# The attention bias in scratch memory laid out so that one read of 128 partitions brings a part of the bias tile for both blocks of rows, the first part read one round sooner

## The chip, the cores and the metric

The kernel runs on one core of a Trainium2 chip. The metric is the device time of one execution in microseconds (us), lower is better. Its engines, as the profile names them: PE (TensorE, matmuls; PEld is its weight loads), DVE (VectorE), ACT (ScalarE), POOL (GpSimd) and SP, which computes nothing here and issues every DMA.

## The reference, cut to what matters

```python
batch, n_heads, seq, head_dim = (4, 8, 576, 64)
...
scores = scale * np.matmul(q, k.transpose(0, 1, 3, 2))
rel = (pos[:, None] - pos[None, :]).astype(np.float32)
x = (np.log1p(np.abs(rel)) / psi_i)[..., None]
h = np.maximum(x @ w1 + b1, 0.0)
bias = h @ w2
scores = scores + bias.transpose(2, 0, 1)[None, :, :, :]
scores = scores - np.max(scores, axis=-1, keepdims=True)
attn = np.exp(scores)
attn = attn / (np.sum(attn, axis=-1, keepdims=True) + 1e-09)
out = np.matmul(attn, v)
```

The bias of a head is a 576 x 576 matrix that a small network computes from the distance of two positions and the row's position; all four batches share it. The attention's output goes through a feed-forward layer (512 to 2048 to 512) and then through a soft mixture of 8 experts; neither is touched here.

## The kernel before, in words

**The bias stage (`bias_phase`, to about 70 us).** The 576 positions of the query are cut into 9 blocks of 64 rows. Blocks c and 8 - c (c = 0 to 3) go as a pair over 128 partitions, one of them on the even and the other on the odd partitions; block 4 goes alone, with its own scratch tensor `W4`. A round k (0 to 8) makes 64 distances: PE multiplies masks with weights (L160), DVE makes of the sums the bias values of 64 distances forwards (L193) and POOL copies them in reverse order for the distances backwards (L211). They collect in SBUF tiles called `rows`, with two heads (a head pair, hp = 0 to 3) interleaved. When the last round of a chunk of distances is done (`CHUNKS`), `put` (L220) sends the chunk to the scratch tensor `W` in HBM, by `send` (L215, the DMA on line L216). `W` holds for each row a line of 1152 distances for each of two heads, so a shifted window of 576 of them is that row's bias. Pair c = 3 is complete after round 5, c = 2 after round 6, c = 1 after round 7 and c = 0 after round 8. For c < 3 the last chunk (for c = 0 also the one before it) is sent for head pair 0 alone, and the rest of it (`late`, 8 DMAs) after everything else.

**The reads.** `bias_rows` (L324) reads the windows back into a bias tile `nb` of 128 partitions and 9 x 576 values: part s (0 to 3) holds the pair c = 3 - s, part 4 the block 4 of both heads. Before, one part takes two DMAs of 64 rows: one of the first block of the pair into the even partitions and one of the other block into the odd ones. For head pair 0 the parts are read one by one (`bias_first`, L349): part 0 and part 4 after round 6, part 1 after round 7, parts 2 and 3 after the last round. For head pairs 1 to 3 `load` (L357) reads all parts when the first batch of that head pair is loaded.

**Attention (`Attention.run`, L544).** There are 16 pairs of head pair and batch. Each has 9 score tiles of 128 x 576, t = 0 to 8: `scores` (L414, PE), `least` (L437, DVE: adds the bias from `nb`, scales and takes the row's minimum of the negated sum, giving z), `power` (L457, ACT: the exponential e), `transposes` (L477, PE) and `gather` (L491 on DVE, L493 on ACT: g), then `pv` (L505, PE) and small sums (`inverse`, L523). `SLOT` says which rows of the bias tile a score tile takes: t = 0 and 1 take part 0, t = 2 and 3 part 1, t = 4 and 5 part 2, t = 6 part 4, t = 7 and 8 part 3. The order is written out in `ROUND`: round i ends pair i and begins pair i + 1. The inputs q and k of pair i + 2 (`raw`, L365) are loaded in round i, and POOL splits them into two parts each (`split`, L382 and L384: qh, kh, ql, kl). PSUM has 4 buffers for score and transposed tiles together, so PE stops where DVE does not take a score tile.

**Queues.** All DMAs go through SP, which works in program order; a DMA whose condition is not met holds all those behind it. Their completions are counted on eight semaphores that are used in turn (DMAHW0 to DMAHW7 below).

Of the kernel before, what the change touches and what calls it, by code (L numbers as in the profile page):

```python
# [8 lines left out]
F32 = mybir.dt.float32  # L9
# [10 lines left out]
P = 128  # L20
B, H, S, D = 4, 8, 576, 64
HP = H // 2
# [15 lines left out]
PITCH = 2 * S  # L38
# [30 lines left out]

def bias_phase(tc, ident, W, W4, cpack, lcol, prow, xmain, xtail, att):  # L70


    nc = tc.nc
    with ExitStack() as ctx:
# [73 lines left out]
        def unit(k, c):  # L148

            if c < 4 or k % 2 == 0:  # L150
                accs[c] = ap_.tile([P, 2, 2, H, 32], F32, tag="acc", name=f"acc{k}_{c}")
            acc = accs[c]
            if c < 4:
                m, cols, dst = P, slice(P * c, P * c + P), acc
            else:
                m, cols = 64 * (k % 2) + 64, slice(512, S)
                dst = acc[m - 64 : m]
            for u in range(16):
                for part in range(3):
                    nc.tensor.matmul(  # L160
                        dst[:, u // 8, :, :, 4 * (u % 8) : 4 * (u % 8) + 4],
                        mask[:, (16 * k + u) % RING, cols],
                        wp[:, part],
                        start=part == 0,
                        stop=part == 2,
                    )
            if c == 4 and k in (0, 2):
                return
            ks = CHUNKS[c]
            i = max(n for n in range(len(ks)) if ks[n] <= k)  # L170
            d0, w, f0 = 64 * ks[i], 64 * (ks[i + 1] - ks[i]), 64 * (k - ks[i])
            last = k + 1 == ks[i + 1]
            if c == 4:
                w, f0, xs = 64, 0, xt_t[:m, i]
            else:
                xs = xm_t[:, k, c]
            if f0 == 0:
                tag = TAGS[c][i]
                rows[c] = fps[tag].tile([P, H * 2 * w], F32, tag=tag, name=f"rows{c}_{i}")
            mine = rows[c]  # L180
            if c == 4:
                both = rows[c].rearrange("p (h x) -> p h x", h=H).unsqueeze(2)
            else:
                both = rows[c].rearrange("p (a x b) -> p a b x", a=HP, b=2)
            fwd = both[:m, :, :, w + f0 : w + f0 + 64]
            tmp = cp.tile([P, H, 2, 32], F32, tag="tmp", name=f"tmp{k}_{c}", bufs=2)
            xb = xs.rearrange("p (s j) -> p s j", s=2).unsqueeze(1).to_broadcast([m, H, 2, 32])
            a0, a1 = (acc[:m, :, n].rearrange("p s h j -> p h s j") for n in range(2))
            nc.vector.tensor_tensor(tmp[:m], a0, xb, ALU.mult)
            if c == 4:  # L190
                nc.vector.tensor_tensor(fwd[:, :, 0].rearrange("p h (s j) -> p h s j", s=2), tmp[:m], a1, ALU.add)
            else:
                nc.vector.tensor_tensor(  # L193
                    fwd.rearrange("p a b (s j) -> p a b s j", s=2),
                    tmp[:m].rearrange("p (a b) s j -> p a b s j", b=2),
                    a1.rearrange("p (a b) s j -> p a b s j", b=2),
                    ALU.add,
                )

            one = d0 == 0 and c < 4  # L200
            z = int(one and f0 == 0)
            a = both[:m, :, :, w + one - f0 - 64 : w + one - f0 - z]
            if c == 4:
                a, src = a[:, :, 0], fwd[:, :, 0]
            else:
                src = fwd[:, :, :, z:]
            e = a.ap[-1][0]
            back = bass.AP(
                tensor=a.tensor, offset=a.offset + (63 - z) * e, ap=[list(v) for v in a.ap[:-1]] + [[-e, 64 - z]]
            )  # L210
            nc.gpsimd.tensor_scalar(back, src, 1.0, 1.0, ALU.mult, ALU.mult)  # L211
            if not last:
                return

            def send(dst, src, pin):  # L215
                i = nc.sync.dma_start(dst, src)  # L216
                if pin:
                    tc.keep_in_program_order(i)

            def put(half, blk, d0, n_r, n_l, one, hs):  # L220

                q = slice(64 * half, 64 * half + 64) if blk == 4 else slice(half, P, 2)
                if blk == 4:
                    e, dst = 1, W4.rearrange("h p j -> p h j")
                else:
                    e = 2
                    dst = W[blk - (blk > 4) if blk > 4 else 3 - blk, hs].rearrange("a p j b -> p a (j b)")
                src = mine.rearrange("p (h x) -> p h x", h=H // e)[:, hs if e == 2 else slice(0, H)]

                def move(j0, x0, n):  # L230
                    send(dst[:, :, e * j0 : e * (j0 + n)], src[q, :, e * x0 : e * (x0 + n)], k > 4)

                if one:
                    move(S - n_l, w - n_l + 1, n_l + n_r - 1)
                    return
                if n_r > 0:
                    move(S - 1 + d0, w, n_r)
                if n_l > 0:
                    y = int(d0 == 0)
                    move(S - d0 - n_l, w - n_l, n_l - y)  # L240

            def flush(hs):
                if c == 4:
                    for half in range(m // 64):
                        put(half, 4, d0 + 64 * half, 64, 64, False, hs)
                else:
                    far, near = min(w, S - 64 * c - d0), max(0, min(w, 64 * c + 64 - d0))
                    put(0, c, d0, far, near, one, hs)
                    put(1, 8 - c, d0, near, far, one, hs)

            if c < 3 and (k + 1 == ks[-1] or c == 0 and i == 2):
                flush(slice(0, 1))
                late.append(lambda: flush(slice(1, HP)))
            else:
                flush(slice(0, HP))
# [8 lines left out]
        for k in range(NG):  # L264
            cs = [c for c in range(3, -1, -1) if k <= NG - 1 - c]
            if k < 5:
                cs.append(4)
            done = 0
            for n_, c in enumerate(cs):
                unit(k, c)  # L270
                if k + 1 < NG:
                    upto = 16 * (n_ + 1) // len(cs)
                    for u in range(done, upto):
                        make_mask(k + 1, u)
                    done = upto
            if k < 4:
                att.split(0, k)
            if k in (6, 7):
                att.bias_first(k - 6)
        att.load(1)  # L280
        att.load_v(1)
        att.bias_first(2)
# [5 lines left out]
class Attention:  # L288
# [17 lines left out]

    def __init__(self, tc, ident, W, W4, xT, rs, qk, v_l):
        self.tc, self.nc, self.ident = tc, tc.nc, ident
# [15 lines left out]
    def bias_rows(self, hp, s, n):  # L324

        nb = self.nb[hp]
        if s == 4:
            parts = [(slice(64 * par, 64 * par + 64), 4) for par in range(2)]
        else:
            parts = [(slice(q, P, 2), s + 5 * q) for q in range(2)]  # L330
        for p, blk in parts:
            i0 = 64 * (blk if blk >= 4 else 3 - blk)
            if s == 4:
                a = self.W4[2 * hp + p.start // 64, :, S - 1 - i0 : 2 * S - 1 - i0]
                src = bass.AP(tensor=a.tensor, offset=a.offset, ap=[[PITCH - 1, 64], [1, S]])
                dst = nb[p, 8 * S :]
            else:
                a = self.W[blk - (blk > 4), hp, :, S - 1 - i0 : 2 * S - 1 - i0]
                step = H * 64 * PITCH + (128 if blk < 4 else -128)
                dims = [[2 * (PITCH - 1), 64], [step, n], [1, 2 * S]]  # L340
                src = bass.AP(tensor=a.tensor, offset=a.offset, ap=[d for d in dims if d[1] > 1])
                dst = nb[p, 2 * S * s : 2 * S * (s + n)]
                if n > 1:
                    dst = dst.rearrange("p (s x) -> p s x", s=n)
            i = self.nc.sync.dma_start(dst, src)
            if hp == 0:
                self.tc.keep_in_program_order(i)
# [824 lines left out]
def kernel(  # L1172
# [1 line left out]
):  # L1174
    nc = tc.nc
    dram = ctx.enter_context(tc.tile_pool(name="scratch", bufs=1, space=DRAM))
    W = dram.tile([8, HP, 64, PITCH, 2], F32, name="W")
    W4 = dram.tile([H, 64, PITCH], F32, name="W4")
    xT = dram.tile([HP, P, N], F32, name="xT")
    rs = dram.tile([H, N], F32, name="rs")  # L1180
# [4 lines left out]
    att = Attention(tc, ident, W, W4, xT, rs, qk, v_l)  # L1185
# [9 lines left out]
    x0 = ctx.enter_context(tc.tile_pool(name="m_x0", bufs=1, reuse_waits="tile"))  # L1195
# [179 lines left out]
```

## Time and profile before

| | |
|---|---|
| time, median of 3 runs | 819.85 us (819.35 to 821.1) |
| the profiled execution's own time | 815.85 us |
| its span, first to last instruction | 813.9 us |
| mean granted clock of TensorE | 0.975 of full speed |
| busy: PE, DVE, ACT, POOL | 759.6, 546.7, 495.1, 314.5 us |
| HBM read and written | 91.95 and 21.29 MB |
| reads of the bias tile | 6 of 1152 KB, 8 of 288 KB, 8 of 144 KB |

PE is busy for 93% of the span and is on the chain that ended last for 45% of it, mostly in the feed-forward layer (L725, L753). In the row of 40 slices (each 20.3 us) PE is at 9 tenths or more nearly everywhere after the first 15% of the span; the one slice before that where it falls to 3 tenths is the fourth, 61 to 81 us, where the bias stage ends and attention begins. The granted clock falls in the same place, and the DMA share there is high.

### The profile page before, as it was taken

How to read it: one execution, taken by the hardware profiler on the slowest of the kernel's cores; microseconds unless marked ns; L12 is line 12 of the kernel's file. 1: busy time of each engine (PE TensorE's matmuls, PEld its weight loads, DVE VectorE, ACT ScalarE, POOL GpSimd, SP SyncE). 2: the span in 40 equal slices, each digit the busy share in tenths (PEclk: the TensorE clock that was granted, in tenths of full speed). 3: DMA queues.
4: the chain of work that ended last, by engine and by line, in shares of the span. 5: the costliest groups of instructions: out<-in, count | busy, mean ns of one | idle time of the engine just before them, and what ended most of it. 6: DMA issues, size and time to landing. Idle time of an engine off the chain costs nothing.

```text
span 813.9 us, 18359 instructions
## 1 busy us (share of the span) xinstructions
PE 759.6 (93%) x7428; PEld 634.7 (78%) x7428; DVE 546.7 (67%) x958; ACT 495.1 (61%) x974; POOL 314.5 (39%) x239
## 2 busy tenths in 40 slices
PE   6993599999999999999999999999999999998993
PEld 6883477787877778988898988888888899886342
DVE  6894688888988856777778565655675656465103
ACT  8980688888888853443346566656566556655002
POOL 4742225375646623113224454445543641141000
PEclk9998799999999999999999999999999999999897
DMA  6596923738535542332340011301100124339986
GB/s 198 168 276 199 372 79 121 272 108 308 171 95 177 181 137 78 140 120 104 104 130 1 1 33 40 136 1 40 39 1 20 39 104 130 104 104 328 384 351 232
DMA packets 49669, 114.44 MB, mean 141 GB/s; under 512 B 10544, under 2 KB 29872, under 8 KB 47536
## 3 DMA queue, kind: packets, MB, share of 16 engines
q1 hardware_dynamic: 49584, 113.26, 41.3%
q8 instruction: 58, 0.95, 0.5%
q14 instruction: 27, 0.22, 0.1%
HBM read 91.95 MB, written 21.29 MB: 139 GB/s over the span
## 4 chain that ended last, share of the span: by engine, by line
PE 45%; DVE 3%; ACT 1%; DMA 1%; POOL 1%; issue 0%; DVEq 0%; ACTq 0%
PE h L725 18%; PE ys L753 18%; PE hps L1136 2%; PE ops L1136 2%; PE lp L823 1%; DMA em<-in_mw_dram 1%; PE turn L1145 1%; PE o L1163 1%; DVE x L644 0%; DVE g L736 0%; PE sp L882 0%; PE sp L883 0%; DVE wr L685 0%; DVE gr L741 0%; PE tl L870 0%
## 5 line engine op out<-in xcount | busy, mean ns | idle before, releaser
L736 DVE SCALAR_TENSOR_TENSOR g<-g,nal 128x384 f32<-128x384 f32 x96 | 100.6, 1048 | 83.9 <-ACT g L735 83.5
L437 DVE CUSTOM_DVE_ANT_0 z<-s,nb 128x576 f32<-128x576 f32 x144 | 108.2, 755 | 26.0 <-DMA W<-rows 12.6
L457 ACT ACTIVATE e<-z,m 128x576 f32<-128x576 f32 x144 | 109.9, 766 | 6.2 <-DVE m L437 6.2
L739 ACT ACTIVATE gr<-g 128x384 fp32r<-128x384 f32 x96 | 50.2, 523 | 86.7 <-DVE g L736 86.6
L505 PE MATMUL o<-g,v 128*64 128x256 f32 (+1 forms) x640 | 86.4, 415 | 0.5 <-ACT g L493 0.5
L493 ACT ACTIVATE g<-t 128x640 f32<-128x640 f32 x96 | 67.2, 702 | 31.1 <-PE t L477 26.8
L733 ACT ACTIVATE g<-h 128x384 f32<-128x384 f32 x96 | 46.8, 488 | 54.5 <-PE h L725 51.4
L414 PE MATMUL s<-kh,qh 64*128 64x288 f32 x320 | 61.3, 379 | 16.4 <-DVE m L437 14.9
L741 DVE TENSOR_TENSOR gr<-g,gr 128x384 fp32r<-128x384 f32 x80 | 53.8, 673 | 33.2 <-ACT gr L739 33.2
L477 PE MATMUL t<-ident,e 64*128 64x64 f32 x1440 | 67.9, 223 | 3.7 <-ACT g L493 3.2
L477 PEld LDWEIGHTS t<-ident,e 64*128 64x128 f32 x1440 | 65.7, 139 | 5.3 <-ACT g L493 3.9
L160 PE MATMUL acc<-wp,mask 128*128 128x64 bf16 (+1 forms) x1680 | 56.4, 197 | 11.2 <-DVE mask L144 5.2
L505 PEld LDWEIGHTS o<-g,v 128*64 128x64 f32 x640 | 43.9, 138 | 29.0 <-ACT g L493 1.0
L160 PEld LDWEIGHTS <-mask 128*128 128x128 bf16 (+1 forms) x1680 | 54.2, 103 | 13.3 <-DVE mask L144 5.2
L142 ACT ACTIVATE mask<-pr,wb 128x576 bf16<-128x576 f16 (+4 forms) x94 | 54.6, 677 | 2.5 <-PE acc L160 2.5
L382 POOL TENSOR_SCALAR qh<-raw 128x1216 fp32r<-128x1216 f32 x16 | 19.4, 1211 | 87.4 <-PE s L414 67.1
L414 PEld LDWEIGHTS s<-kh,qh 64*128 64x128 f32 x320 | 31.1, 190 | 25.4 <-DVE m L437 15.6
L741 POOL TENSOR_TENSOR gr<-g,gr 128x384 fp32r<-128x384 f32 x16 | 19.1, 1194 | 77.8 <-ACT gr L739 39.3
L414 PE MATMUL s<-kl,qh 64*128 64x288 f32 x320 | 48.0, 295 | 0.0
L414 PE MATMUL s<-kh,ql 64*128 64x288 f32 x320 | 47.8, 294 | 0.0
L735 ACT ACTIVATE g<-h 128x384 f32<-128x384 f32 x96 | 46.5, 485 | 0.0
L384 POOL TENSOR_TENSOR ql<-raw,qh 128x1216 fp32r<-128x1216 f32 x16 | 44.8, 2801 | 0.0
(990 smaller groups left out, 2016.7 us busy)
## 6 DMA issues: line engine op xcount, KB each, us to landing
wide<-in_w_dram SPq DMA_DIRECT2D x16, 1024.0 KB
ep<-in_mw_dram SPq DMA_DIRECT2D x29, 512.0 KB
raw<-in_qk_dram SPq DMA_DIRECT2D x16, 896.0 KB
nb<-W SPq DMA_DIRECT2D x6, 1152.0 KB
v<-in_v_l_dram SPq DMA_DIRECT2D x16, 320.0 KB
pre<-in_mw_dram SPq DMA_DIRECT2D x10, 512.0 KB
ex<-in_mw_dram SPq DMA_DIRECT2D x9, 512.0 KB
em<-in_mw_dram SPq DMA_DIRECT2D x8, 512.0 KB
```

Source lines behind the costliest of these rows:

```text
L142: nc.scalar.activation(dst, pr[:, :n], AF.Sigmoid, bias=wb[:, t : t + 1], scale=BIG)
L160: nc.tensor.matmul(dst[:, u // 8, :, :, 4 * (u % 8) : 4 * (u % 8) + 4], mask[:, (16 * k + u) % RING, cols], wp[:, part], start=part == 0, ...
L414: nc.tensor.matmul(s[:, hf, :288], st["q", a][d, o : o + P], st["k", b][d, 288 * h : 288 * h + 288], start=n_ == 0, stop=n_ == len(seq) - 1,),
L437: self.nc.vector.tensor_tensor_reduce(out=z.rearrange("p (a b) -> p a b", a=2), in0=s[:, :, :288], in1=nb.rearrange("p (a b) -> p a b", a= ...
L457: self.nc.scalar.activation(e, z, AF.Exp, bias=m, scale=-1.0, accum_out=st["sum"][:, slot : slot + 1]),
L477: self.pin(i, nc.tensor.transpose(tp[:, r, 64 * c : 64 * c + 64], e[q, k0 : k0 + P], self.ident[q, q]))
L493: self.pin(i, nc.scalar.activation(dst, src, AF.Copy))
L505: nc.tensor.matmul(op[64 * h : 64 * h + 64, 0, :n], st["v"][:, h, c], g[:, h, c], start=c == 0, stop=c == 4),
L725: nc.tensor.matmul(h, w_[:, c * P : (c + 1) * P], x_[:, c], start=c == 0 and n_ == 0, stop=c == NC - 1 and n_ == 2,)
L736: nc.vector.scalar_tensor_tensor(g, neg, self.nal[:, f : f + 1], g, ALU.mult, ALU.add)
L741: eng.tensor_tensor(gl, g, gh.bitcast(F32), ALU.subtract)
L753: i = self.nc.tensor.matmul(self.ys[blk][t], g_[:, t * P : (t + 1) * P], w_[:, 512:], start=f == 0 and n_ == 0, stop=f == NF - 1 and n_ == 2,)
```

## The change

It lays `W` out anew: for each pair c and head pair 128 lines of 2304 values, in the order of the partitions, so that the lines of the two blocks alternate. The line of the second block is shifted by 256 (4 - c) - 1 values (an odd number of words), so that a window that moves back by one value from one line to the next fits both blocks. Then one DMA of 128 rows reads one part. `put` writes into every second line. `bias_first(0)` is called after round 5 in place of round 6, so part 0 and part 4 are read one round sooner; the other parts stay where they were.

```diff
@@ put @@
-                    e, dst = 1, W4.rearrange("h p j -> p h j")
+                    e, odd, dst = 1, 0, W4.rearrange("h p j -> p h j")
                 else:
-                    e = 2
-                    dst = W[blk - (blk > 4) if blk > 4 else 3 - blk, hs].rearrange("a p j b -> p a (j b)")
+                    e, odd = 2, half * (256 * (4 - c) - 1)
+                    dst = W[3 - c, hs, half::2].rearrange("a p j -> p a j")
...
-                    send(dst[:, :, e * j0 : e * (j0 + n)], src[q, :, e * x0 : e * (x0 + n)], k > 4)
+                    send(dst[:, :, e * j0 + odd : e * (j0 + n) + odd], src[q, :, e * x0 : e * (x0 + n)], k > 4)
@@ the rounds @@
-            if k in (6, 7):
-                att.bias_first(k - 6)
+            if k in (5, 7):
+                att.bias_first(k // 7)
@@ bias_rows, parts 0 to 3 @@
-                a = self.W[blk - (blk > 4), hp, :, S - 1 - i0 : 2 * S - 1 - i0]
-                step = H * 64 * PITCH + (128 if blk < 4 else -128)
-                dims = [[2 * (PITCH - 1), 64], [step, n], [1, 2 * S]]
+            x0 = 2 * (S - 1 - 64 * (3 - s))
+            a = self.W[s, hp, :, x0 : x0 + 2 * S]
+            dims = [[2 * PITCH - 1, P], [HP * P * 2 * PITCH + P, n], [1, 2 * S]]
...
-                dst = nb[p, 2 * S * s : 2 * S * (s + n)]
+            dst = nb[:, 2 * S * s : 2 * S * (s + n)]
@@ the scratch tensor @@
-    W = dram.tile([8, HP, 64, PITCH, 2], F32, name="W")
+    W = dram.tile([4, HP, P, 2 * PITCH], F32, name="W")
```

In the order of the built program PE, DVE, ACT and POOL keep theirs through attention and the feed-forward layer. Three places matter here. In the names, `rows3_2` is the third chunk of pair c = 3, `W_57` is `W`, `W4_58` is `W4`, `nb0` the bias tile of head pair 0, and the brackets give what the instruction waits for.

SP, the end of round 5 and round 6, before:

```order
L216 DMA W_57<-rows3_2_1363 64x4x256 [waits DMAHW6_49]
L216 DMA W_57<-rows1_2_1478 64x4x256 [waits DMAHW7_49,Pool_49]
L216 DMA W_57<-rows1_2_1478 64x4x256 [waits DMAHW0_49]
L216 DMA W_57<-rows2_2_1711 64x256 [waits DMAHW1_49,Pool_49]
L216 DMA W_57<-rows2_2_1711 64x256 [waits DMAHW2_49]
L216 DMA W_57<-rows0_2_1535 64x384 [waits DMAHW3_49,Pool_49]
L216 DMA W_57<-rows0_2_1535 64x384 [waits DMAHW4_49]
L345 DMA nb0_2016<-W_57 64x1152 [waits DMAHW5_49]
L345 DMA nb0_2016<-W_57 64x1152 [waits DMAHW6_49]
L345 DMA nb0_2016<-W4_58 64x576 [waits DMAHW7_49]
```

and with the change:

```order
L216 DMA W_57<-rows3_2_1363 64x4x256 [waits DMAHW6_49]
L216 DMA W_57<-rows1_2_1478 64x4x256 [waits DMAHW7_49,Pool_49]
L216 DMA W_57<-rows1_2_1478 64x4x256 [waits DMAHW0_49]
L343 DMA nb0_1836<-W_57 128x1152 [waits DMAHW6_49,DMAHW5_49,DMAHW1_49]
L343 DMA nb0_1836<-W4_58 64x576 [waits DMAHW4_49,DMAHW3_49,DMAHW2_49]
L343 DMA nb0_1836<-W4_58 64x576
L216 DMA W_57<-rows2_2_1711 64x256 [waits Pool_49]
L216 DMA W_57<-rows2_2_1711 64x256
L216 DMA W_57<-rows0_2_1535 64x384 [waits Pool_49]
```

The two DMAs of part 0 became one, and it and those of part 4 now stand ahead of the four writes of round 6. It waits for the two writes of `rows3_2`, the last of pair c = 3.

SP, from the writes of round 7 to the last reads, before:

```order
L216 DMA W_57<-rows1_3_1945 64x256 [waits DMAHW1_49,Pool_49]
L216 DMA W_57<-rows1_3_1945 64x256 [waits DMAHW2_49]
L345 DMA nb0_2016<-W_57 64x1152 [waits DMAHW3_49]
L345 DMA nb0_2016<-W_57 64x1152 [waits DMAHW4_49]
L216 DMA W_57<-rows0_3_2133 64x256 [waits DMAHW5_49,Pool_49]
L216 DMA W_57<-rows0_3_2133 64x256 [waits DMAHW6_49]
L345 DMA nb0_2016<-W_57 64x1152 [waits DMAHW7_49,DMAHW1_49]
L345 DMA nb0_2016<-W_57 64x1152 [waits DMAHW2_49,DMAHW0_49]
L345 DMA nb0_2016<-W_57 64x1152 [waits DMAHW5_49]
L345 DMA nb0_2016<-W_57 64x1152 [waits DMAHW6_49]
L216 DMA W_57<-rows2_2_1711 64x3x256 [waits DMAHW3_49]
```

and with the change:

```order
L216 DMA W_57<-rows1_3_1949 64x256 [waits DMAHW0_49,Pool_49]
L216 DMA W_57<-rows1_3_1949 64x256 [waits DMAHW1_49]
L343 DMA nb0_1836<-W_57 128x1152 [waits DMAHW5_49,DMAHW4_49,DMAHW2_49]
L216 DMA W_57<-rows0_3_2132 64x256 [waits DMAHW3_49,Pool_49]
L216 DMA W_57<-rows0_3_2132 64x256
L343 DMA nb0_1836<-W_57 128x1152 [waits DMAHW1_49,DMAHW0_49]
L343 DMA nb0_1836<-W_57 128x1152 [waits DMAHW6_49,DMAHW7_49,DMAHW4_49,DMAHW3_49]
L216 DMA W_57<-rows2_2_1711 64x3x256 x2
```

Each part is one read; the read of part 1 still stands behind the writes of `rows1_3`, that of part 2 behind those of `rows0_3`, and that of part 3 waits for the latter.

DVE, the first tiles of attention (the z of pair 0), before:

```order
L437 ISA z0_0_2264,m0_0_2265<-s0_0_2257,nb0_2016 128x576 [waits DMAHW3_49,DMAHW4_49,DMAHW2_49,DMAHW5_49,DMAHW1_49,DMAHW6_49,DMAHW0_49,DMAHW7_49,PE_49,Activation_49]
L437 ISA m0_0_2265 128x1
L437 ISA z0_1_2274,m0_1_2275<-s0_1_2267,nb0_2016 128x576 [waits PE_49]
L437 ISA m0_1_2275 128x1
L437 ISA z0_2_2286,m0_2_2287<-s0_2_2277,nb0_2016 128x576 [waits PE_49]
L437 ISA m0_2_2287 128x1
L437 ISA z0_3_2300,m0_3_2301<-s0_3_2291,nb0_2016 128x576 [waits PE_49]
L437 ISA m0_3_2301 128x1
L437 ISA z0_4_2310,m0_4_2311<-s0_4_2303,nb0_2016 128x576 [waits PE_49]
```

and with the change:

```order
L435 ISA z0_0_2260,m0_0_2261<-s0_0_2253,nb0_1836 128x576 [waits DMAHW1_49,PE_49,Activation_49]
L435 ISA m0_0_2261 128x1
L435 ISA z0_1_2270,m0_1_2271<-s0_1_2263,nb0_1836 128x576 [waits PE_49]
L435 ISA m0_1_2271 128x1
L435 ISA z0_2_2282,m0_2_2283<-s0_2_2273,nb0_1836 128x576 [waits DMAHW2_49,PE_49]
L435 ISA m0_2_2283 128x1
L435 ISA z0_3_2296,m0_3_2297<-s0_3_2287,nb0_1836 128x576 [waits PE_49]
L435 ISA m0_3_2297 128x1
L435 ISA z0_4_2306,m0_4_2307<-s0_4_2299,nb0_1836 128x576 [waits DMAHW5_49,PE_49]
L435 ISA m0_4_2307 128x1
L435 ISA z0_5_2329,m0_5_2330<-s0_5_2309,nb0_1836 128x576 [waits PE_49]
L435 ISA m0_5_2330 128x1
```

Before, the first z waits for all eight DMA semaphores, and the next ones for none. Now the first waits for one, that of the read of part 0; the z of t = 2 and t = 4 each wait for one more, that of their own part, and so do those of part 4 and part 3 behind them.

## Rows read from the trace of the kernel before

**Rows 1.** The bias tile's instructions, what they wait for (all of the span).

```profile
L437 DVE CUSTOM_DVE_ANT_0 z<-s,nb x144: 697/758/760, 82.8 to 293.1; 128x576 f32<-128x576 f32 x144
L345 SPq DMA_DIRECT2D nb<-W x22: 451/601/1332, 68.5 to 197.5; - x22
...
  DMA W<-rows: 12.6, 1
```

**Rows 2.** DVE's instructions in order: start us, us, line, tiles, [idle <-releaser].

```profile
69.52 0.69 DVE L193 TENSOR_TENSOR rows<-tmp,acc 128x512 f32<-128x512 f32 x1
...
82.79 0.76 DVE L437 CUSTOM_DVE_ANT_0 z<-s,nb 128x576 f32<-128x576 f32 x1 [12.59 <-DMA W<-rows]
...
85.51 0.75 DVE L437 CUSTOM_DVE_ANT_0 z<-s,nb 128x576 f32<-128x576 f32 x1
...
91.53 0.75 DVE L437 CUSTOM_DVE_ANT_0 z<-s,nb 128x576 f32<-128x576 f32 x1
...
93.22 2.52 DVE L523 SCALAR_TENSOR_TENSOR r<-sum 128x9 f32<-128x9 f32 x1 [0.94 <-ACT e L457]
...
95.90 0.70 DVE L437 CUSTOM_DVE_ANT_0 z<-s,nb 128x576 f32<-128x576 f32 x1
...
111.36 0.76 DVE L437 CUSTOM_DVE_ANT_0 z<-s,nb 128x576 f32<-128x576 f32 x1
...
124.38 0.76 DVE L437 CUSTOM_DVE_ANT_0 z<-s,nb 128x576 f32<-128x576 f32 x1
```

**Rows 3.** Busy us of each engine by stretch, then granted clock, DMA share, GB/s.

```profile
42.00:60.00 18.00, 16.30 (x525) 15.60 (x522) 17.34 (x38) 16.19 (x35) 7.08 (x11) 1.00 0.96 268
...
74.00:82.00 8.00, 0.00 (x0) 0.00 (x0) 0.00 (x0) 0.00 (x0) 0.00 (x0) 0.50 0.88 288
82.00:87.00 5.00, 2.97 (x26) 2.63 (x28) 4.16 (x12) 3.37 (x6) 0.00 (x0) 0.50 1.08 330
...
98.00:102.00 4.00, 3.79 (x28) 2.48 (x30) 0.69 (x3) 2.37 (x6) 0.00 (x0) 0.59 1.05 352
```

**Rows 4.** SP's DMAs in order: start, us of issuing, line, tiles.

```profile
61.21 2.27 SPq L216 DMA_DIRECT2D W<-rows  x2
...
73.90 1.17 SPq L216 DMA_DIRECT2D W<-rows  x2
...
77.00 1.09 SPq L345 DMA_DIRECT2D nb<-W  x2
78.13 5.84 SPq L216 DMA_DIRECT2D W<-rows  x8
84.01 0.69 SPq L365 DMA_DIRECT2D raw<-in_qk_dram  x1
...
165.05 1.82 SPq L623 DMA_DIRECT2D xb<-rs  x2
```

**Rows 5.** POOL's instructions in order, as rows 2.

```profile
68.37 1.29 POOL L211 TENSOR_SCALAR rows<-rows 128x512 f32<-128x512 f32 x2 [1.08 <-DVE rows L193]
70.29 0.67 POOL L211 TENSOR_SCALAR rows<-rows 128x512 f32<-128x512 f32 x1 [0.62 <-DVE rows L193]
91.15 1.21 POOL L382 TENSOR_SCALAR qh<-raw 128x1216 fp32r<-128x1216 f32 x1 [20.20 <-PE s L414]
...
92.97 2.74 POOL L384 TENSOR_TENSOR ql<-raw,qh 128x1216 fp32r<-128x1216 f32 x1
95.67 1.41 POOL L384 TENSOR_TENSOR kl<-raw,kh 128x576 fp32r<-128x576 f32 x1
...
169.57 1.02 POOL L634 TENSOR_TENSOR xu<-xu,xb 128x384 f32<-128x384 f32 x1 [1.09 <-DMA xb<-rs]
```

**Rows 6.** ACT's instructions in order, as rows 2.

```profile
88.73 0.76 ACT L457 ACTIVATE e<-z,m 128x576 f32<-128x576 f32 x1
...
89.48 0.68 ACT L493 ACTIVATE g<-t 128x640 f32<-128x640 f32 x1
```

**Rows 7.** Line L523 in all pairs: min/median/max ns of one.

```profile
L523 DVE SCALAR_TENSOR_TENSOR r<-sum x16: 166/718/2517, 93.2 to 295.3; 128x9 f32<-128x9 f32 x16
```

More of the change, by code (lines that the diff above doesn't have):

```diff
@@ L326, in bias_rows @@
         nb = self.nb[hp]
+        jobs = []
         if s == 4:
-            parts = [(slice(64 * par, 64 * par + 64), 4) for par in range(2)]
-        else:
[L330 to L337, printed above, removed]
-                a = self.W[blk - (blk > 4), hp, :, S - 1 - i0 : 2 * S - 1 - i0]
-                step = H * 64 * PITCH + (128 if blk < 4 else -128)
-                dims = [[2 * (PITCH - 1), 64], [step, n], [1, 2 * S]]
-                src = bass.AP(tensor=a.tensor, offset=a.offset, ap=[d for d in dims if d[1] > 1])
-                dst = nb[p, 2 * S * s : 2 * S * (s + n)]
-                if n > 1:
-                    dst = dst.rearrange("p (s x) -> p s x", s=n)
+            for par in range(2):
+                a = self.W4[2 * hp + par, :, S - 1 - 256 : 2 * S - 1 - 256]
+                src = bass.AP(tensor=a.tensor, offset=a.offset, ap=[[PITCH - 1, 64], [1, S]])
+                jobs.append((nb[64 * par : 64 * par + 64, 8 * S :], src))
+        else:
+            x0 = 2 * (S - 1 - 64 * (3 - s))
+            a = self.W[s, hp, :, x0 : x0 + 2 * S]
+            dims = [[2 * PITCH - 1, P], [HP * P * 2 * PITCH + P, n], [1, 2 * S]]
+            src = bass.AP(tensor=a.tensor, offset=a.offset, ap=[d for d in dims if d[1] > 1])
+            dst = nb[:, 2 * S * s : 2 * S * (s + n)]
+            if n > 1:
+                dst = dst.rearrange("p (s x) -> p s x", s=n)
+            jobs.append((dst, src))
+        for dst, src in jobs:
             i = self.nc.sync.dma_start(dst, src)
```

## The prediction

> **What bounds the kernel now.** I read four views in this order. First what the bias tile waits for [rows 1]: 144 z instructions on DVE read it, and one single wait of 12.6 us stands before them, put down to a DMA. Then DVE in order of time [rows 2]: DVE ends the bias stage at 69.52 + 0.69 = 70.21, and the first z starts at 82.79, after 12.59 us of idle time. The table by stretch [rows 3] shows that this is a hole in the whole kernel: from 74 to 82 no engine does anything, the DMA queue is busy at a share of 0.88, and TensorE's granted clock is 0.50 of full speed, the lower level of 1.2 GHz; it is still 0.50 from 82 to 87, when PE works again. Last SP's order [rows 4]: the last two reads of the bias tile are issued from 77.00 to 78.09, then the eight late writes, then `raw` of pair 2 at 84.01.
>
> The built order says what the first z waits for: before, all eight DMA semaphores, which covers the ten reads of all parts, though it needs part 0 alone. The next z's wait for no DMA, and they do follow each other without a gap (82.79 to 85.51 are four z's in 2.7 us [rows 2]). So the start of attention is set by the last read, not by the first. With the change the first z waits for one read. That is what the time should come from; the fewer DMAs as such matter less.
>
> **The change part by part.**
>
> *When part 0 is there.* Its read stands behind the writes of round 5, whose issue ends at 61.21 + 2.27 = 63.48 [rows 4], and waits for writes that were issued a few us sooner. How long a write takes to land: the read at 77.00 waited for the first of the writes issued from 73.90 [rows 4], so 3.1 us at most there. The queue was fuller in 42 to 60 (share 0.96 [rows 3]), so the read may go out at 63.5, or up to 2 us later. How long a 128-row read takes no row shows. Below: the second `xb` read, issued at 165.05 + 1.82 - 0.6 = 166.27 [rows 4], released POOL at 169.57 [rows 5], 3.3 us for a much smaller read. Above: the second of the last reads, issued at about 77.5 [rows 4], was followed by z at 82.79 [rows 2], 5.3 us with writes beside them. I take 4.0, nearer the lower end, because at 63.5 little else is in the queue. Part 0 is there at 67.5 (66.8 to 70.8), and the first z can start when DVE is free, at 70.3: 12.5 us sooner (12.0 at the worst end).
>
> *Parts 1 to 3.* They now pace the first pair. POOL ends the rows of round 7 by 69.66 and those of round 8 at 70.96 [rows 5]. SP writes the former from 69.0 to 70.2, then issues the read of part 1: landed at 74.2. It writes the latter to 72.1; the read of part 2 waits for the writes of round 7 (69.6 + 3.1 = 72.7): landed at 76.7. The read of part 3 waits for the writes of round 8 (71.6 + 3.1 = 74.7): landed at 78.7. Each may be 0.7 us less or 1.3 us more.
>
> *To the end of pair 0's z's.* The first z of part 2 is at 76.7 instead of 85.51 [rows 2]. Its second ends at 78.2, and ACT, which now keeps up, computes the sixth e (0.76 us, before at 88.73 [rows 6]) to 79.0. From the end of that e at 89.49 (where ACT's g follows, then PE's transposes and its last score tile) the last z took 2.04 us before, to 91.53. So the last z is at 81.0, later than part 3 needs: **10.5 us sooner**.
>
> *The gap before pair 1.* Before, DVE's r at 93.22 took 2.52 us, while the median of r is 0.72 [rows 2, 7]; POOL's ql ran from 92.97 to 95.71 [rows 5] and r ended with it. With the change POOL cannot be there yet, since it waits for `raw` of pair 2 (below). That gives back 1.8 us (2.35 at most, by the shortest r of 0.17): **1.8 us**, so that pair 1's first z is at 83.6 rather than 95.90.
>
> *Pair 1.* Before, pair 1 took 111.36 - 95.90 = 15.46 us where pair 2 took 124.38 - 111.36 = 13.02 [rows 2]. The excess of 2.4 lies where the clock fell once more (0.59 in 98 to 102 [rows 3]). Whether it falls again is open: the gain is 0 to 2.4, and I take **1.2**, half.
>
> *`raw` of pair 2.* The late writes follow the last read, now at 74.7 and 0.6 us long instead of to 78.09: `raw` is issued some 2.8 us sooner, at 81.2. Before, POOL started on it at 91.15, waiting for PE's last score of pair 0 and not for the DMA [rows 5], so it lands at most 7.1 us after its issue: by 88.3. POOL's four splits take 97.08 - 91.15 = 5.93, to 94.3, and pair 2's first z can follow a score tile later, some 95.1. The sum puts it at 111.36 - 13.5 = 97.9, so this does not bind; it caps the gain at 16.3.
>
> *The rest.* The other head pairs' reads are three DMAs instead of four, each hidden: pair 4 needs its bias 26 us after pair 2 starts. From pair 2 on the rounds are 13 us and the orders are the same, so what is gained by pair 2's first z is kept to the end. Writes are as many and as long as before; that they go to every second line I cost at nothing, which the fourth rival below takes up.
>
> Sum: 10.5 + 1.8 + 1.2 = **13.5 us**. The profiled execution's own time, 815.85, becomes 802.35. The median of the runs, 819.85, stands 4.0 above it and includes the same hole; taken off there, 806.35, say **806.3 us**.
>
> A rule speaks for another sum. The trace's part first: the two reads of a part were issued one after the other, each by itself, and z waited for the last of ten [rows 1, 4]. The Trainium skill (DMA: Bandwidth & Descriptors, Rules for kernel authors) says that two transfers to disjoint halves of the partitions serialise, because both use the same 16 engines, and that one transfer of 128 partitions should be used. By that rule the merged read moves the same bytes over the same engines and saves an issue, some 0.6 us each, about 2 us of SP's time up to the last read; the sum would be 2 to 3 us. It says nothing of what a reader waits for, and the order does.
>
> **The rivals.**
>
> *The clock stays low and the first pair starves.* The z's come in twos, each two behind a read, so PE works in short bursts from 71 to 79. For it: the clock was at 0.50 after one hole of 12 us and fell to 0.59 again when PE was only partly busy before 98 [rows 3]. At half clock the score tile and transposes ahead of the last z cost some 1 us more, part 1 to 3 may each come 1.3 late, and pair 1 keeps its 15.46: 10.5 - 2.3 + 1.8 = 10, so 809.9. The Trainium skill (TensorE: Matmul & The Clock Gate, HAM oscillation) describes such a loop of bursts and DMA waits, with the clock low again at each burst. The trace agrees as far as a long hole goes; no row shows short ones.
>
> *The first z is held by the writes, as the view names them.* The idle time is put down to W<-rows, not to the reads. If the eight late writes hold z, the change moves them only as far as the last read, 2.8 to 3.3 us: 816.8. Against it: in the order z waits for nothing that stands behind the reads; the semaphores are used in turn by reads and writes, which is how the name can be wrong.
>
> *More is gained.* Pair 1 runs at 13 us and r at its shortest: up to the cap of 16.3, 803.5.
>
> *Slower: the odd lines cost.* The second block's runs now begin at an odd word and go to every second line. The queue is busy 0.96 of the 18 us from 42 to 60 [rows 3], in which SP issued nothing but writes of `W` and `W4`. If the second block's half of them took twice as long, 0.96 x 18 / 2 = 8.6 us would be added there, and half of the 5.84 of the late writes [rows 4], 2.9: 11.5 against a gain of 13.5, still 2 us faster. It decides from a factor of 2.2; at three times it is 23 - 13.5 = 9.5 slower, 829. No row excludes it, but the reads of block 4 already step by an odd number of words, and nothing waits for them alone.
>
> **How the numbers follow.** Forecast (10.5 to 15 us gained): 0.67. Low clock (8.5 to 10.5): 0.15. Writes hold z: 0.06. More than 15: 0.07. Odd lines at twice the time or more: 0.05, of it 0.02 within what can be told and 0.03 slower. The range takes in the first, most of the second and the larger gains up to 18 (cap 16.3 and the spread of the runs, 1.7): 801.8 to 811.4. A change of under 0.2%, 1.6 us, can't be told from none here: faster by more 0.95, within 0.02, slower 0.03.
>
> **What would show it.** The first z at 70 to 71 us; gaps before the z's of t = 2 and 4, at about 74 and 77, put down to reads of the bias tile; the last z of pair 0 near 81, pair 1's first near 83.6 with an r under 1 us, pair 2's first near 98, then rounds of 13.0; no stretch without work from 74 to 82. It is wrong if the first z is still behind 75, if the DMA share before 60 gives longer writes and the bias stage itself ends later than 70.2, or if POOL's first split after 70 us waits for `raw` to after 91.

## The result and the profile after

| | before | with the change |
|---|---|---|
| time, median of the runs | 819.6 us (819.05 to 821.1, 4 runs) | 809.01 us (808.39 to 810.13, 4 runs) |
| ratio | | 0.9869, interval 0.9852 to 0.9887 |
| the profiled execution, its span | 815.85, 813.9 us | 808.88, 807.1 us |
| mean granted clock | 0.975 | 0.974 |

The change gains 10.6 us by the medians; 13.5 were forecast. The two profiled executions stand only 7.0 us apart. That is because the one of before lies 3.75 us under its median, and the one of after lies on its own. Lines of the attention stand two lower in the new code: z is L435 for L437, r is L521 for L523, POOL's ql is L382 for L384.

The bias tile's instructions over all of the span, for [rows 1]:

```profile
L435 DVE CUSTOM_DVE_ANT_0 z<-s,nb x144: 696/757/761, 75.1 to 287.9; 128x576 f32<-128x576 f32 x144
L343 SPq DMA_DIRECT2D nb<-W x15: 326/507/1291, 67.7 to 191.4; - x15
...
  DMA nb<-W: 6.1, 3
```

One wait of 12.6 us became three that sum to 6.1 us. DVE in order of time, for [rows 2], shows where they lie:

```profile
74.48 0.69 DVE L193 TENSOR_TENSOR rows<-tmp,acc 128x512 f32<-128x512 f32 x1
75.09 0.75 DVE L435 CUSTOM_DVE_ANT_0 z<-s,nb 128x576 f32<-128x576 f32 x1
...
80.12 0.76 DVE L435 CUSTOM_DVE_ANT_0 z<-s,nb 128x576 f32<-128x576 f32 x1 [3.60 <-DMA nb<-W]
...
83.14 0.76 DVE L435 CUSTOM_DVE_ANT_0 z<-s,nb 128x576 f32<-128x576 f32 x1 [1.58 <-DMA nb<-W]
...
86.92 0.76 DVE L435 CUSTOM_DVE_ANT_0 z<-s,nb 128x576 f32<-128x576 f32 x1 [0.92 <-DMA nb<-W]
88.34 0.75 DVE L435 CUSTOM_DVE_ANT_0 z<-s,nb 128x576 f32<-128x576 f32 x1
...
90.03 0.17 DVE L521 SCALAR_TENSOR_TENSOR r<-sum 128x9 f32<-128x9 f32 x1 [0.94 <-ACT e L455]
...
90.37 0.70 DVE L435 CUSTOM_DVE_ANT_0 z<-s,nb 128x576 f32<-128x576 f32 x1
...
105.95 0.76 DVE L435 CUSTOM_DVE_ANT_0 z<-s,nb 128x576 f32<-128x576 f32 x1
...
118.98 0.76 DVE L435 CUSTOM_DVE_ANT_0 z<-s,nb 128x576 f32<-128x576 f32 x1
```

The first z follows the last instruction of the bias stage without a wait; the z of t = 2, 4 and 7 each wait for their part. The bias stage itself ends at 74.48 + 0.69 = 75.17 instead of 70.21. So the two profiles are best compared from the end of that stage: pair 2's first z comes 30.8 us behind it (105.95 - 75.17) where it came 41.2 behind it. From pair 2 to pair 3 it is 13.0 us in both.

So the 6.8 us between the spans are + 5.0 (end of the bias stage), - 10.4 (from there to pair 2), + 0.2 (from there to the last z, at 287.9 for 293.1) and - 1.6 (behind it).

The stretches of [rows 3], with 87 to 96 added and the last one begun 2 us sooner: busy us of each engine, granted clock, DMA share, GB/s.

```profile
42.00:60.00 18.00, 13.91 (x437) 13.34 (x437) 15.40 (x31) 13.42 (x26) 5.87 (x9) 1.00 0.98 254
74.00:82.00 8.00, 4.20 (x48) 3.54 (x50) 3.93 (x10) 3.99 (x8) 1.31 (x2) 0.81 0.64 190
82.00:87.00 5.00, 3.83 (x40) 3.17 (x40) 2.94 (x8) 3.52 (x9) 0.00 (x0) 0.50 0.94 307
87.00:96.00 9.00, 8.56 (x80) 6.61 (x80) 5.19 (x14) 6.00 (x13) 0.00 (x0) 0.50 1.02 236
96.00:102.00 6.00, 6.00 (x102) 5.14 (x100) 4.26 (x11) 3.86 (x8) 4.95 (x4) 1.00 0.91 365
```

The stretch without work is gone, but the granted clock is at 0.50 (1.2 GHz) from 82 to 96. SP's order, for [rows 4]:

```profile
67.74 1.60 SPq L343 DMA_DIRECT2D nb<-W  x3
...
76.14 0.33 SPq L343 DMA_DIRECT2D nb<-W  x1
...
77.77 3.46 SPq L343 DMA_DIRECT2D nb<-W  x2
81.28 6.08 SPq L216 DMA_DIRECT2D W<-rows  x8
88.48 0.34 SPq L363 DMA_DIRECT2D raw<-in_qk_dram  x1
```

And POOL's first split of pair 2, for [rows 5], with the same split in the run `part1_sooner` (below) behind it:

```profile
97.05 1.21 POOL L380 TENSOR_SCALAR qh<-raw 128x1216 fp32r<-128x1216 f32 x1 [21.12 <-PE o L503]
```

```profile
95.83 1.22 POOL L380 TENSOR_SCALAR qh<-raw 128x1216 fp32r<-128x1216 f32 x1 [21.84 <-DMA raw<-in_qk_dram]
```

It starts six us later than before. The first row names PE's o, but in the built order this split waits for two things only: the load of `raw`, and a matmul of pair 0's last score tile, which PE had done by 88. So it waited for `raw`, issued at 88.48 and there 8.6 us later, as the second row says of its run (86.98 to 95.83, 8.9 us). Before, it took 7.1 us at most [rows 4, 5].

### The profile page after: what moved, and what is told of

It is laid out like the page before. It is cut to its first block, busy times and chain, and to the rows that moved or that the text cites. A ratio compares the mean times of both kernels' runs of the same rounds, so it can differ in the third digit from the quotient of the medians.

```text
span 807.1 us, 18353 instructions
## 1 busy us (share of the span) xinstructions
PE 763.2 (95%) x7428; PEld 638.1 (79%) x7428; DVE 548.2 (68%) x958; ACT 495.7 (61%) x974; POOL 314.6 (39%) x239
## 4 chain that ended last, share of the span: by engine, by line
PE 45%; DVE 4%; ACT 1%; DMA 1%; POOL 1%; issue 1%; DVEq 0%; ACTq 0%
PE ys L751 18%; PE h L723 18%; PE ops L1134 2%; PE hps L1134 2%; PE lp L821 1%; DMA em<-in_mw_dram 1%; PE turn L1143 1%; PE sp L880 1%; PE sp L881 0%; DVE x L642 0%; DVE g L734 0%; DVE wr L683 0%; DVE gr L739 0%; PE tc L930 0%; PE tl L868 0%
## 5 line engine op out<-in xcount | busy, mean ns | idle before, releaser
L435 DVE CUSTOM_DVE_ANT_0 z<-s,nb 128x576 f32<-128x576 f32 x144 | 108.2, 755 | 18.7 <-PE s L412 9.7
L160 PE MATMUL acc<-wp,mask 128*128 128x64 bf16 (+1 forms) x1680 | 58.3, 200 | 15.0 <-issue 6.0
L160 PEld LDWEIGHTS <-mask 128*128 128x128 bf16 (+1 forms) x1680 | 56.4, 104 | 16.8 <-DVE mask L144 5.3
L382 POOL TENSOR_TENSOR ql<-raw,qh 128x1216 fp32r<-128x1216 f32 x16 | 44.8, 2802 | 0.0
```

The costliest lines, as they stand in the source:

```text
L160: nc.tensor.matmul(dst[:, u // 8, :, :, 4 * (u % 8) : 4 * (u % 8) + 4], mask[:, (16 * k + u) % RING, cols], wp[:, part], start=part == 0, ...
L435: self.nc.vector.tensor_tensor_reduce(out=z.rearrange("p (a b) -> p a b", a=2), in0=s[:, :, :288], in1=nb.rearrange("p (a b) -> p a b", a= ...
```

## The experiments

"Behind the stage" is always the time from the end of the last L193 to the z named, in one profiled execution.

### The two halves of the change, apart

`layout_only` is the change with part 0 read after round 6, as before:

```diff
-            if k in (5, 7):
-                att.bias_first(k // 7)
+            if k in (6, 7):
+                att.bias_first(k - 6)
```

> The new layout and its reads of 128 partitions, but part 0 and part 4 read after round 6 as before. Theory W (the gain comes from what the first z waits for): the first z still waits for one read only, but that read goes out behind the writes of round 6, some 4 to 5 us later than in the change, and z starts about 4 us after it, so the gain over before falls from 10.6 us to 6 to 9: 811 to 814 us, and the first z is still ahead of the read of part 3. Theory E (the gain comes from reading one round sooner): hardly anything is left, 817 to 820 us.

`early_only` is the kernel before with the opposite edit: old layout, two DMAs to a part, part 0 read after round 5.

> The kernel before with its layout and its reads of 64 rows, only with part 0 and part 4 read after round 5. Theory W: the first z still waits for the last read, which moves by at most the time that SP issues four reads, so 817 to 820 us, with an idle DVE of about 10 to 12 us before the first z. Theory E: 809 to 812 us, as the change.

Measured: `layout_only` 808.14 us, ratio 0.9857 (0.9816 to 0.9898). `early_only` 817.44, ratio 0.9968 (0.9944 to 0.9992). DVE in order of time in `layout_only`, last of the bias stage, first and last z of pair 0, first of pairs 1 and 2:

```profile
72.58 0.69 DVE L193 TENSOR_TENSOR rows<-tmp,acc 128x512 f32<-128x512 f32 x1
75.47 0.76 DVE L435 CUSTOM_DVE_ANT_0 z<-s,nb 128x576 f32<-128x576 f32 x1 [2.20 <-PE s L412]
...
86.50 0.75 DVE L435 CUSTOM_DVE_ANT_0 z<-s,nb 128x576 f32<-128x576 f32 x1
...
88.53 0.70 DVE L435 CUSTOM_DVE_ANT_0 z<-s,nb 128x576 f32<-128x576 f32 x1
...
102.59 0.76 DVE L435 CUSTOM_DVE_ANT_0 z<-s,nb 128x576 f32<-128x576 f32 x1
```

and in `early_only` the first z:

```profile
70.90 0.69 DVE L193 TENSOR_TENSOR rows<-tmp,acc 128x512 f32<-128x512 f32 x1
83.20 0.76 DVE L437 CUSTOM_DVE_ANT_0 z<-s,nb 128x576 f32<-128x576 f32 x1 [11.61 <-DMA W<-rows]
```

The layout with its reads of 128 partitions gives the whole gain, more than either theory left it (811 to 814 us at best). Without the sooner read the first z starts 2.2 us behind the stage, but the last z of pair 0 is 13.2 us behind it (86.50 - 73.27), just as with the change (88.34 - 75.17 = 13.2). Part 0 isn't what pair 0 ends on; parts 1 to 3 are. In the old layout the sooner read leaves a wait of 11.6 us (12.6 before) and gains 0.3%, since the first z still waits for all reads: theory W.

### What a z waits for, and the merged read

Two kernels keep the new layout and read each part by two DMAs of 64 rows again, `halves_adj` into partitions 0 to 63 and 64 to 127, `halves_alt` into the even and the odd ones. In the built order the first z waits for the two reads of its own part in the first kernel and for the reads of all parts in the second.

```diff
-            dims = [[2 * PITCH - 1, P], [HP * P * 2 * PITCH + P, n], [1, 2 * S]]
+            for q in range(2):
+                dims = [[2 * PITCH - 1, 64], [HP * P * 2 * PITCH + P, n], [1, 2 * S]]
+                off = a.offset + 64 * q * (2 * PITCH - 1)
...
+                dst = nb[64 * q : 64 * q + 64, 2 * S * s : 2 * S * (s + n)]
```

(`halves_adj`; `halves_alt` has `2 * (2 * PITCH - 1)` for the step, `q * (2 * PITCH - 1)` for the offset and `nb[slice(q, P, 2), ...]`.)

> The change, but each part is read by two DMAs of 64 rows, into partitions 0 to 63 and 64 to 127: as many DMAs as before, and the first z waits for its own two reads. Theory W: as the change within 1 us, 808 to 811 us. Theory M (merging the reads, fewer and larger DMAs, is what gains): 815 to 820 us.

> The change, but each part is read by two DMAs of 64 rows into the even and into the odd partitions: the same number of DMAs and bytes as with adjacent halves, but the first z waits for all reads again, by the order of the built program. Theory W: the gain is gone, 816 to 821 us, with the first z behind the last read. Theory M: the same as with adjacent halves.

Measured: `halves_adj` 812.81 us, ratio 0.9916 (0.9887 to 0.9945); `halves_alt` 820.29, ratio 1.0001 (0.9972 to 1.0031), nothing gained at all. The second is as theory W has it, the first lies between the two theories. DVE in `halves_alt`, the bias stage's last and the first z:

```profile
72.02 0.69 DVE L193 TENSOR_TENSOR rows<-tmp,acc 128x512 f32<-128x512 f32 x1
87.68 0.76 DVE L437 CUSTOM_DVE_ANT_0 z<-s,nb 128x576 f32<-128x576 f32 x1 [14.97 <-DMA W<-rows]
```

The two kernels issue the same number of DMAs over the same bytes; they differ in which partitions each fills, and so in what z waits for. That is 7.5 us between their medians. In `halves_adj` the first z is at 74.25, as the stage ends (73.64 + 0.69 = 74.33), in `halves_alt` 15.0 us behind it. Not all of the 15.0 is the wait for the other parts: in `halves_adj` all reads had landed by 11.5 us behind the stage, where the z of t = 7 starts without waiting for its own. The other 3.4 us are reads that were issued later (the last by 9.0 us behind the stage for 7.5) and took longer to land, and no run says why. `halves_adj` gives back some 3 us later: its pairs 5 and 6 take 15.1 and 14.2 us for 13.0, and there PE waits for POOL's split (PE in order of time):

```profile
157.29 0.46 PE L414 MATMUL s<-kl,qh 64*128 64x288 f32 x2 [1.69 <-POOL kl L384]
```

The Trainium skill (DMA: Bandwidth & Descriptors, Rules for kernel authors) advises one transfer of 128 partitions over two halves. By the medians one read beats the adjacent halves by 3.8 us. That the halves serialise isn't shown by it: pair 2 starts 29.6 us behind the stage with the halves and 30.8 with the change, and 3.3 us are lost in pairs 5 and 6. The sharing of engines isn't where most of the gain is from.

### Does the clock hold pair 0?

`warm` adds 36 matmuls behind the sixth score tile of pair 0, into columns of its PSUM tile that nothing reads, so that PE stays busy in the gaps.

```diff
+        if i == 0 and t == 5:
+            for n_ in range(36):
+                d = slice(64 * (n_ % 2), 64 * (n_ % 2) + 64)
+                nc.tensor.matmul(
+                    s[:, n_ % 2, 288:512], st["q", 0][d, 0:P], st["k", 0][d, 0:224], start=True, stop=True
+                )
```

> The change with 36 extra matmuls on PE after the sixth score tile of pair 0, where PE waits for the read of part 1; they write columns that nothing reads. Theory C (the low clock after that wait is what makes pairs 0 and 1 long): the granted clock stays at 1.0 through 78 to 96 us, pair 1 takes 13 to 14 us instead of 15.6 and the time falls by 2 to 3 us, to 806 to 807. If the pace is set by the reads and by DVE and ACT alone: no change, 808 to 810 us.

Measured: 808.6 us, ratio 0.9861 (0.9827 to 0.9895). The table by stretch (columns as above):

```profile
78.00:82.00 4.00, 2.49 (x44) 2.19 (x40) 1.44 (x4) 2.25 (x6) 0.00 (x0) 1.00 0.92 280
82.00:86.00 4.00, 2.17 (x24) 1.62 (x24) 2.86 (x7) 2.63 (x8) 0.00 (x0) 0.63 0.90 309
86.00:90.00 4.00, 4.00 (x48) 3.84 (x46) 2.22 (x6) 2.28 (x7) 0.00 (x0) 0.52 1.14 256
```

The clock is held at 1.00 over the first gap (0.61 in the same stretch with the change alone) and falls behind it all the same. The last z of pair 0 is 13.2 us behind the stage, as without the extra work, and the time is within the range of "no change". So the first gap comes from the read, not from a slow PE, and the rows name reads before the other two. What the clock would give if it were held throughout, which is theory C, this run doesn't tell.

### The lines in HBM

`line_2305` and `line_2320` change the length of a line of `W`, so that the step of the reads is 2304 or 2319 instead of 2303 values.

```diff
+LINE = 2305
...
-            dims = [[2 * PITCH - 1, P], [HP * P * 2 * PITCH + P, n], [1, 2 * S]]
+            dims = [[LINE - 1, P], [HP * P * LINE + P, n], [1, 2 * S]]
...
-    W = dram.tile([4, HP, P, 2 * PITCH], F32, name="W")
+    W = dram.tile([4, HP, P, LINE], F32, name="W")
```

> The change with lines of 2305 instead of 2304 values in W, so that the second block's runs begin at an even word again and the same block's lines are 18440 bytes apart, no multiple of 1 KB. Theory O (the new layout makes the writes of W slower, by the odd word or by the distance of the lines): the bias stage's last DVE instruction ends at 70 to 72 us as with the old layout, not at 73 to 75, the DMA queue moves 275 to 290 GB/s per full share from 42 to 60 us instead of 247 to 259, and the time falls by 2 to 4 us below the change, to 805 to 807. Theory N (the bias stage's end is scatter from run to run): no change, 808 to 810 us.

> The change with lines of 2320 values: the lines of one block are 18560 bytes apart instead of 18432, but the second block's runs still begin at an odd word. Theory O by the distance of the lines: as with 2305, 805 to 807 us. Theory O by the odd word: as the change, 808 to 810 us and 247 to 259 GB/s per full share.

`before_again` is the kernel before once more, for a second profile of it. `old_odd` is the kernel before with one thing of the new layout: the second block's lines begin one word later.

```diff
-                    e = 2
-                    dst = W[blk - (blk > 4) if blk > 4 else 3 - blk, hs].rearrange("a p j b -> p a (j b)")
+                    e, odd = 2, half
+                    dst = W[blk - (blk > 4) if blk > 4 else 3 - blk, hs].rearrange("a p j -> p a j")
```

> The kernel before once more, unchanged. Theory O: its bias stage ends at 70 to 72 us again and the DMA queue moves 275 to 290 GB/s per full share from 42 to 60 us. Theory N: it may end anywhere from 70 to 75 us.

> The layout, the reads and the waits of before, but the second block's lines begin one word later, so that its writes start at an odd word. Theory A, the odd word slows the writes of W: GB/s divided by the DMA share in 42 to 60 us falls from 279 to 298 (three runs of the old layout) to about 250, as in the new layout; the bias stage ends about 2.5 us later than its old mean of 71.6, at 74, and the time is 821 to 823 us. Theory B, it is the place of the lines (every second one) and not the odd word: that quotient stays at 279 or more, and the time is 819 to 820.5 us. Either way the first z still waits for all reads and pair 2's first z comes 41 to 44 us after the stage's end.

Measured: `line_2305` 808.19 us, ratio 0.9853 (0.9826 to 0.988); `line_2320` 808.99, ratio 0.9867 (0.9841 to 0.9894); `before_again` 822.15 in its one execution; `old_odd` 820.33 beside 820.27 of before, ratio 1.0 (0.9976 to 1.0023). The stretch from 42 to 60 in `before_again`, `old_odd`, `line_2305` and `line_2320`, and in `both_sooner` (below, with lines of 2305), in this order:

```profile
42.00:60.00 18.00, 14.55 (x468) 14.11 (x469) 15.80 (x32) 13.59 (x27) 6.90 (x11) 1.00 0.86 256
```

```profile
42.00:60.00 18.00, 14.59 (x422) 14.19 (x419) 14.45 (x30) 13.68 (x26) 5.88 (x9) 0.91 0.96 243
```

```profile
42.00:60.00 18.00, 15.66 (x506) 15.16 (x503) 16.91 (x34) 14.03 (x28) 7.19 (x11) 1.00 0.99 264
```

```profile
42.00:60.00 18.00, 13.92 (x440) 13.37 (x438) 15.60 (x31) 13.35 (x26) 5.88 (x9) 1.00 1.00 253
```

```profile
42.00:60.00 18.00, 14.48 (x415) 14.01 (x411) 14.66 (x31) 13.26 (x26) 5.86 (x9) 0.91 0.94 262
```

GB/s divided by the share of the DMA engines' time says how fast the writes go while they go. Old layout: 268/0.96 = 279 [rows 3], 256/0.86 = 298, and 288 in `early_only`. With the change: 254/0.98 = 259. One odd word in the old layout: 243/0.96 = 253. With lines of 2305 values the second block's shift and its odd line number add up to an even word, so no line begins at an odd one: 264/0.99 = 267, and 262/0.94 = 279 in `both_sooner`. `line_2320`, another distance of the lines with odd starts, is at 253. Over all profiles it is 242 to 259 in the nine with odd starts and 267 to 298 in the five without. So writes go slower where there are odd starts, by some 10%. It isn't that the lines alternate: they don't in `old_odd`. No cost in time is shown: `old_odd` has the median of before within 0.24% either way, so up to 2 us could hide there, and `line_2305` is at theory N's time, 0.8 us from the change, within what the runs scatter. Theory A had the slower writes right and its 821 to 823 us wrong.

The stage's end is a poor witness here. It is 70.2 in the first profile of before and 73.0 in the second; 71.6 in `early_only`; 74.9 in `old_odd`; 72.7 to 75.2 in the ten profiles of the new layout, of which the two with even starts have 72.8 and 75.2. In the new layout it is no sooner with even starts.

### Sooner still

`part1_sooner` reads part 1 after round 6, ahead of the writes of round 7:

```diff
-            if k in (5, 7):
-                att.bias_first(k // 7)
+            if k in (5, 6):
+                att.bias_first(k - 5)
```

> Part 1 is read after round 6 instead of round 7. Theory A, the last z of pair 0 is set by part 3, whose writes come from the last round: the first gap (3.6 us before the z of t = 2) shrinks to under 1 us, the later gaps grow, the last z of pair 0 stays 12 to 13 us after the stage's end, and the time is 808 to 809.5 us. Theory B, each read queues behind the one ahead of it, so a sooner part 1 makes parts 2 and 3 sooner too: the last z of pair 0 comes 10 to 11 us after the stage's end, and the time is 806 to 807 us.

`raw_sooner` issues the loads of pair 2 ahead of the eight late writes (and leaves them out of round 0):

```diff
+        att.load(2)
+        att.load_v(2)
...
-                if t == 0 and i + 2 < np_:
+                if t == 0 and 2 < i + 2 < np_:
```

> The inputs of pair 2 are loaded ahead of the eight late writes instead of behind them. Theory A, they do not bind: the splits of pair 2 start some 6 us sooner (about 91 instead of 97), pair 2's first z stays 29 to 31 us after the stage's end, and the time is 808 to 809.5 us. Theory B, POOL's splits of pair 2 and the transfers beside them hold pair 1: pair 2's first z comes 27 to 28 us after the stage's end, and the time is 806 to 807 us.

`both_sooner` has both edits and lines of 2305 values.

> The two edits together, with lines of 2305 values (so that the reads step by 2304). If each of them only moves a wait, 807.5 to 809 us, like the line of 2305 alone (808.2). If parts 2 and 3 and the splits of pair 2 follow sooner, 805 to 806 us, the best of all kernels.

Measured in one batch, before at 820.27 us: `part1_sooner` 809.92, ratio 0.9873 (0.9857 to 0.989); `raw_sooner` 811.41, ratio 0.9883 (0.9867 to 0.9899); `both_sooner` 813.08, ratio 0.9913 (0.9888 to 0.9938). None is better than the change; `both_sooner`, outside both of its ranges, is worse. SP and then DVE in `part1_sooner`:

```profile
69.53 3.35 SPq L216 DMA_DIRECT2D W<-rows  x4
74.33 0.33 SPq L343 DMA_DIRECT2D nb<-W  x1
75.17 2.37 SPq L216 DMA_DIRECT2D W<-rows  x4
78.90 0.83 SPq L343 DMA_DIRECT2D nb<-W  x2
```

```profile
78.48 0.76 DVE L435 CUSTOM_DVE_ANT_0 z<-s,nb 128x576 f32<-128x576 f32 x1 [3.90 <-DMA nb<-W]
...
83.15 0.76 DVE L435 CUSTOM_DVE_ANT_0 z<-s,nb 128x576 f32<-128x576 f32 x1 [3.23 <-DMA nb<-W]
```

Neither theory foresaw the first of these: the wait of t = 2 does not shrink. The read stands at the head of SP's queue until the writes of round 6 have landed (issued by 72.88, the read at 74.33) and holds the writes of rounds 7 and 8 behind it. All parts are late: the last z of pair 0 is 14.8 us behind the stage.

In `raw_sooner` both theories were wrong too. The splits start 7.5 us sooner than with the change, 5.1 if counted from the stage's end, and pair 2 begins 33.6 us behind the stage instead of 30.8. Of that 1.5 us are pair 0, whose last z is at 14.7 for 13.2, and 1.3 are pair 1, which takes 16.9 us for 15.6 (14.1 in `part1_sooner`). PE in `raw_sooner` and then in `part1_sooner`, the last matmuls of pair 0's output:

```profile
92.53 4.53 PE L505 MATMUL o<-g,v 128*64 128x256 f32 x20
```

```profile
92.86 2.38 PE L503 MATMUL o<-g,v 128*64 128x256 f32 x20
```

The granted clock from 92 to 94 is 0.50 in the first and 1.00 in the second. In `both_sooner` the splits meet r, POOL first and DVE behind it:

```profile
90.50 2.76 POOL L385 TENSOR_TENSOR ql<-raw,qh 128x1216 fp32r<-128x1216 f32 x1
```

```profile
90.69 2.60 DVE L524 SCALAR_TENSOR_TENSOR r<-sum 128x9 f32<-128x9 f32 x1 [0.94 <-ACT e L458]
```

r ends at 93.29, ql at 93.26, as it was before the change [rows 2, 5]; where POOL isn't there r takes 0.17. The Trainium skill (SBUF — State Buffer, SBUF: two separate sides) describes it as a port pair that DVE and GpSimd hold for a whole instruction, so that the loser waits to its end; the trace agrees.

## Why the prediction was right, and where it was off

The time is 2.7 us above the 806.3 that were forecast. By the steps of the forecast, all counted from the end of the bias stage:

- **What bounds the kernel: right.** The first z was held by the reads of all parts, not by that of its own. `halves_alt` has the new layout and that wait, and gains nothing; `halves_adj` has as many DMAs as before, but waits for its own part alone, and gains 6.6 us (819.42 - 812.81). The rival in which the late writes hold z is out: the first z waits for nothing.
- **Part 0 and the first z: right, and worth less than it looked.** z starts as DVE ends the bias stage. But the sooner read that makes it so is worth nothing, as `layout_only` shows; the forecast did say that parts 1 to 3 pace the pair.
- **Parts 1 to 3: the term that was too small.** It had the three z's that wait for a part 4.0, 6.5 and 8.5 us behind the stage; they came 4.95, 7.97 and 11.75 behind it, and the last z 13.2 instead of 10.8. Part 1 was issued 1.0 late and landed within 3.98 us (76.14 to 80.12), the 4.0 that was taken. Part 2, issued at 77.77, took up to 5.37, and part 3, issued at 77.77 + 3.46 - 0.33 = 80.90, up to 6.02. The 4.0 had been chosen for a read with little else in the queue, which holds for part 0; that of part 2 goes out right behind the writes of round 8, that of part 3 right ahead of the late writes. The upper row (5.3 us) had writes beside it, and should have been taken for them. Which transfers slow them no run shows. The path was off too: the last z was forecast to come "later than part 3 needs", and the z of t = 7 waits 0.92 us for part 3. That makes 2.4 us, 1.5 by part 2 and 0.9 by part 3.
- **The gap before pair 1: right.** r took 0.17 instead of 2.52, since POOL was not there. From the last z to pair 1's first it is 2.03 for 4.37, so 2.3 instead of 1.8. `both_sooner` brings POOL back and r is at 2.60 again.
- **Pair 1: open, and it goes with the clock.** 1.2 was taken; the profile shows none of it, 15.6 us. In `layout_only` (102.59 - 88.53), `line_2305`, `line_2320`, `halves_adj` and `part1_sooner` it is 14.1; in `warm`, `halves_alt` and `both_sooner` 15.8, in `raw_sooner` 16.9. The trace shows most of the difference in the last matmuls of pair 0's output: 3.62 us with the change, where the clock is at 0.50 until 96, and 2.38 at 1.00 in `part1_sooner`. Why the clock is up by then in some executions wasn't settled.
- **`raw` of pair 2: right that it doesn't bind, but nearer than forecast.** It was issued 13.3 us behind the stage for 11.0 and took 8.6 us to land for 7.1 at most, so POOL's first split does wait for `raw` to after 91, which the forecast had named as a sign that it is wrong. The splits end at 103.05 (101.61 + 1.44), and DVE goes from pair 1's last z to pair 2's first at 105.95 without a gap. Loaded sooner it gains nothing: in `both_sooner` its splits meet r, in `raw_sooner` pairs 0 and 1 are longer; that the splits or the load are the cause there isn't shown.
- **The odd lines: costed at nothing without a row for it, and they cost nothing that the time shows.** The sign that was named for them came, slower writes before 60 and a stage that ends at 75.2. But the factor on the writes is some 1.1, far from the 2.2 of the slower rival, and the stage ends as late with even starts.
- **The offset of 4.0 to the median** was taken over as it stood. It lay in the stretch at hand: in `before_again`, at 822.15, the bias stage ends 2.8 us later than in the first profile, and pair 2 starts 43.6 us behind it instead of 41.2. So the hole to be closed was larger in this second execution than in the first profiled one.

The sum with what was measured: 27.7 us forecast from the stage's end to pair 2, + 2.4 for the parts, - 0.6 for the gap before pair 1, + 1.3 for pair 1, gives the 30.8 measured.

Of the rivals the low clock with a starved first pair (809.9) came nearest, and its marks are all there: z's in twos behind reads, the clock at 0.50, pair 1 unchanged. Its cause is only half right. `warm` lifts the clock over the first gap and the waits stay: it is the reads that starve the pair. The measured gain of 10.6 us stands at the lower edge of the forecast's 10.5 to 15, next to this rival's 8.5 to 10.5, so the time alone doesn't tell the two apart.

## What to carry to other kernels

Before counting DMAs, read in the built order what the first reader of a tile waits for. Two DMAs into interleaved partitions made the first z wait for all reads of the tile; with one DMA a part, or adjacent halves, it waited for its own. A read moved up in a queue is only worth something if its part is the last to be missed, and it holds all that stands behind it until what it waits for has landed.

## What was not expected of the hardware

The bias stage of one unchanged kernel ended at 70.2 us in one execution and at 73.0 in another. Writes of 4-byte values to HBM went some 10% slower where half of the lines began at an odd word (242 to 259 GB/s per full share against 267 to 298), without the time showing it. And with the change the granted clock stayed at 0.50 (1.2 GHz, the lower of its two levels) from 87 to 96 us although PE was busy for 8.56 of those 9 us.
